# Keeping VectorE off the port it shares with GpSimd: operand places, engine choice and a new order in a fused attention and MLP kernel

## The chip, the cores and the metric

The kernel runs on one core of a Trainium2 chip. The metric is the device time of one execution in microseconds; for the kernel before, three runs gave 625.87, 627.99 and 629.17 us, with a median of 627.99 us. A profile was taken of a further execution.

Five engines work in parallel, each through its own queue in program order: TensorE (PE, with its weight loads shown as PEld), VectorE (DVE), ScalarE (ACT), GpSimd (POOL) and SyncE (SP), which here issues all transfers between HBM and SBUF. Products go to tiles in PSUM, of which the kernel keeps eight; here VectorE and ScalarE read them, and no GpSimd instruction does. Everything else lies in SBUF.

## The reference

The input x has 2048 rows of 512 values. Two blocks follow one another, each with a layer norm that is scaled and shifted by rows computed from a condition vector c.

```python
mod = (silu(c) @ w_mod).reshape(1, 6, 1, 512)      # sa, ca, ga, sb, cb, gb
h = layernorm(x) * (1 + ca) + sa
x = x + ga * A(h)
h = layernorm(x) * (1 + cb) + sb
x = x + gb * B(h)

def A(h):                                           # 32 heads of 16
    q, k, v = split(h @ wqkv)
    phi_q = concat(softmax(q @ w_phi), softmax(-(q @ w_phi)))    # per head, 32 features
    phi_k = concat(softmax(k @ w_phi), softmax(-(k @ w_phi)))
    o = (phi_q @ (phi_k.T @ v)) / (phi_q @ sum(phi_k) + 1e-6)
    return o @ wo

def B(h):
    g = gelu(layernorm(h) @ w1)                     # 512 wide
    x1 = h + shift(g) @ w2                          # quarters shifted by +1, -1, +2, -2 rows
    return x1 + gelu(layernorm(x1) @ w3) @ w4       # 1376 wide
```

## The kernel before, in words

The rows are worked on in tiles of 128. Matrix products run with each operand split into a rounded high part and a rest (`hi_lo`), and three products per pair of parts (`three`); the high part is a copy on ScalarE, and the rest is a subtraction, on VectorE or GpSimd.

There are three stages, which overlap at their edges:

- **Stage 1**, eight chunks of 256 rows. `h_chunk` normalises two tiles (`layernorm2`, from the second chunk on), transposes them on TensorE and splits them. `k_feat` and `v_feat` project keys and values, `q_feat` the queries, each with a softmax of both signs. Keys: `k_feat` divides the exponentials by their sums (tile `ke`), `kv_add` multiplies them with the values into the PSUM tile `kva` and adds the tiles up in `zacc`, a constant tile that the profile calls `const`. Queries: `q_feat` turns 32 by 32 blocks of the PSUM result into the SBUF tile `qt`, forms maximum and minimum, subtracts them into `qe`, and stores `qe` to HBM.
- **Stage 2**, `phase_a` and `mix`, eight chunks. `q_phi` loads a query tile (`e`), multiplies it with the summed keys (`ez`), forms the denominators in small tiles, scales `e` and turns it into `pT`; then come the products with `kvb` (`num`), with `wo`, two norms (`moments`), `w1` with a gelu (`gf`, `sh`), and, for the chunk before, `w2`. Between the stages, `zacc` goes through a product with ones, whose result `zbc` every `ez` needs.
- **Stage 3**, `phase_b`, four blocks of 512 rows: a norm, `w3` with a gelu in eleven column blocks (`up`), `w4` (`down`), and the sum with the two residuals (`xb`, `xc`).

No order is written by hand. `Plan` records every instruction with its cost, its tiles and its alternatives on other engines, and then `order` runs a list scheduler over all of them: at each step it takes, over the engines, the instruction that can start first; among those within a window the smallest number of program position plus `PRIO` of its group. `PICK` and `BIAS` add a handicap to an engine where an instruction may run on two, `CAP` limits how many tiles of a name live at once, `SLOTS` how many buffers of a size there are. What comes out is fixed at build time: which engine, and which place in its queue. Groups are named by part and tile ("h5" is the norm and split of chunk 5, "k11" the keys of tile 11, "z" the summed keys).

The scheduler knows one resource besides the engines and the buffers. An operation marked `lock`, and every GpSimd operation, waits for a variable `port` and then holds it:

```python
            if o.lock:
                port = end - (140 if o.eng == "Pool" else 0)
```

On VectorE that mark is set for `tensor_tensor` and `scalar_tensor_tensor` with both tensors in SBUF, for `tensor_scalar` of more than one element per row with input and output in SBUF, and for the VectorE alternative of an `act` between SBUF tiles. Each of these touches a line that the profile names: L397 and L399 are `tt` on VectorE and GpSimd, L407 `ts`, L415 `stt`, L420 `red`, L423 `recip`, L382 every `act`, L389 its alternatives, L538 and L522 the reciprocal square roots on GpSimd, L703 `turn`, L426 and L430 loads and stores, L447 and L456 products and transposes.

The norm of a pair of tiles (`moments`, then the caller) is a chain over three engines: sums of rows on ScalarE; `nm`, minus the mean, on VectorE; the sums of squares on ScalarE; `mv`, the variance, on VectorE; the root `rs` on GpSimd; `nm` times `rs` on VectorE; and the normalised tile on ScalarE.

## Time and profile before

| | |
|---|---|
| median of three runs | 627.99 us (625.87 to 629.17) |
| the profiled execution, device time | 632.06 us |
| its span, first to last instruction | 630.3 us |
| busy: PE, DVE, ACT, POOL | 602.3, 394.1, 290.3, 289.4 us |
| instructions: DVE, ACT, POOL | 715, 523, 234 |
| mean granted TensorE clock | 0.981 |
| moved through HBM | 47.78 MB read, 20.97 MB written |

The profiled execution is 1.8 us longer than its own span and 4.1 us longer than the median run. The span falls into a start (0 to 21 us, until the large products begin), stage 1 (to about 187 us, where the first `num` product starts), stage 2 (to about 373 us) and stage 3. A row of a timeline gives start, duration, engine, line, operation, tiles and shapes; "x8" is eight instructions in a row, and the bracket says how long the engine had been idle and what ended that. Two products are recorded for each product of two float32 operands.

### The profile page before, as it was taken

Reading aid. Unit: us, or ns where it says so; the run is one execution under the profiler, and the core shown is the slowest. Engines: PE = TensorE matmul, PEld = TensorE weight load, DVE = VectorE, ACT = ScalarE, POOL = GpSimd, SP = SyncE. Lnnn points to the kernel's source line nnn. Section 1 sums busy time; section 2 is a strip of 40 time slices with the busy share of each in tenths; the row PEclk is TensorE's granted clock in tenths of the full one; section 3 lists DMA queues with packets and bytes.
Section 4 is the critical chain, followed back from the end, with each engine's and each line's share of the span. In section 5 each row is a group of like instructions: output and inputs, shape, how many; then the busy total and the mean of one; then the engine's idle time right before and its main releaser. Section 6 shows DMA issues by size and latency. Waiting matters only on the chain.

```text
span 630.3 us, 9391 instructions
## 1 busy us (share of the span) xinstructions
PE 602.3 (96%) x3528; PEld 508.0 (81%) x3528; DVE 394.1 (63%) x715; ACT 290.3 (46%) x523; POOL 289.4 (46%) x234
## 2 busy tenths in 40 slices
PE   4999989998989999898998999999999999999997
PEld 4788868887878777686787988988888898888885
DVE  5689999888999999999975569314511321112112
ACT  3999477733333684553565565323422222221130
POOL 3358985597587689575445673100700060002000
PEclk9699999999999999999999899999999999999999
DMA  8853532201165525551354575102500140003001
GB/s 290 295 159 98 204 105 77 74 1 51 68 234 181 189 105 188 182 174 53 118 167 124 162 238 187 34 1 80 171 1 0 58 145 0 1 1 116 1 0 68
DMA packets 33854, 69.37 MB, mean 110 GB/s; under 512 B 4144, under 2 KB 4784, under 8 KB 33808
## 3 DMA queue, kind: packets, MB, share of 16 engines
q1 hardware_dynamic: 33808, 68.76, 32.7%
q8 instruction: 28, 0.46, 0.3%
q14 instruction: 18, 0.15, 0.1%
HBM read 47.78 MB, written 20.97 MB: 109 GB/s over the span
## 4 chain that ended last, share of the span: by engine, by line
PE 64%; DVE 21%; DMA 5%; ACT 4%; issue 3%; POOL 2%; SPq 1%; DVEq 0%; POOLq 0%
PE pp L447 39%; PE pa L447 22%; DMA xl<-dram 2%; DVE q L420 2%; DVE k L420 2%; PE pt L456 2%; DVE pz L420 2%; DVE pT L703 1%; DVE nm L407 1%; DVE ke L397 1%; DVE e L397 1%; ACT xn L382 1%; PE kva L447 1%; POOL w L399 1%; DVE q L415 1%
## 5 line engine op out<-in xcount | busy, mean ns | idle before, releaser
L447 PE MATMUL pp<-w,gg 128*128 128x512 f32 (+1 forms) x528 | 129.9, 396 | 0.4 <-DVE gg L397 0.4
L397 DVE TENSOR_TENSOR gg<-g,gg 128x512 fp32r<-128x512 f32 (+1 forms) x44 | 33.7, 766 | 152.1 <-ACT gg L382 152.1
L447 PEld LDWEIGHTS pp<-w,gg 128*128 128x128 f32 (+1 forms) x528 | 97.7, 188 | 22.8 <-DVE gg L397 0.8
L447 PE MATMUL pp<-w,hh 128*128 128x512 f32 x384 | 96.3, 407 | 0.9 <-ACT hh L382 0.9
L382 ACT ACTIVATE g<-pa 128x512 f32<-128x512 f32 (+1 forms) x44 | 26.2, 597 | 147.9 <-PE pa L447 147.9
L399 POOL TENSOR_TENSOR xb<-xb,gb 128x512 f32<-128x512 f32 x15 | 20.3, 1354 | 153.1 <-DMA xb<-dram 113.0
L447 PEld LDWEIGHTS pp<-w,hh 128*128 128x128 f32 x384 | 73.1, 194 | 19.0 <-issue 1.3
L447 PEld LDWEIGHTS pa<-bH,w 128*128 128x128 f32 (+1 forms) x528 | 64.9, 186 | 1.8
L447 PE MATMUL pa<-bH,w 128*128 128x256 f32 (+1 forms) x528 | 65.7, 281 | 0.0
L447 PE MATMUL pa<-bT,w 128*128 128x512 f32 (+1 forms) x264 | 64.3, 393 | 0.0
L447 PEld LDWEIGHTS pa<-bT,w 128*128 128x128 f32 (+1 forms) x264 | 48.8, 185 | 11.9
L447 PEld LDWEIGHTS pa<-nT,w 128*128 128x128 f32 x384 | 48.8, 195 | 3.9 <-issue 1.9
L447 PE MATMUL pa<-nT,w 128*128 128x256 f32 x384 | 50.9, 290 | 0.4 <-DVE nT L397 0.4
L447 PE MATMUL pp<-hh,w 128*128 128x256 f32 x384 | 49.2, 284 | 0.0
L447 PEld LDWEIGHTS pp<-hh,w 128*128 128x128 f32 x384 | 47.3, 189 | 2.1 <-issue 1.1
L447 PE MATMUL pp<-w,sh 128*128 128x512 f32 x192 | 48.8, 399 | 0.1
L447 PE MATMUL pp<-w,oT 128*128 128x512 f32 x192 | 47.6, 395 | 0.0
L399 POOL TENSOR_TENSOR w<-raw,w 128x512 fp32r<-128x512 f32 x26 | 36.3, 1403 | 16.6 <-ACT w L382 15.8
L447 PEld LDWEIGHTS pp<-w,sh 128*128 128x128 f32 x192 | 34.8, 188 | 9.0 <-issue 1.3
L447 PEld LDWEIGHTS pp<-w,oT 128*128 128x128 f32 x192 | 35.1, 188 | 7.9 <-issue 0.8
L399 POOL TENSOR_TENSOR e<-e,q 128x1024 f32<-128x1024 f32 x13 | 26.3, 2024 | 25.3 <-DVE q L397 25.2
L399 POOL TENSOR_TENSOR ez<-e,const 128x1024 f32<-128x1024 f32 x15 | 36.1, 2408 | 1.2 <-ACT const L382 0.9
(130 smaller groups left out, 1005.5 us busy)
## 6 DMA issues: line engine op xcount, KB each, us to landing
xl<-in_x SPq DMA_DIRECT2D x32, 256.0 KB, 3.3
dram<-qe SPq DMA_DIRECT2D x16, 512.0 KB, 2.9
e<-dram SPq DMA_DIRECT2D x16, 512.0 KB, 4.5
raw<-in_w SPq DMA_DIRECT2D x26, 256.0 KB, 3.2
mod<-in_wmod SPq DMA_DIRECT2D x24, 256.0 KB, 4.7
dram<-xl SPq DMA_DIRECT2D x16, 256.0 KB, 2.1
xc<-dram SPq DMA_DIRECT2D x16, 256.0 KB, 4.0
dram<-h SPq DMA_DIRECT2D x16, 256.0 KB, 2.7
```

Source lines behind the costliest of these rows:

```text
L382: nc.scalar.activation(o(), i(), func, **kw)
L397: dve = ("DVE", 71 + 1.04 * o.n, lambda: nc.vector.tensor_tensor(o(), a(), b(), op=op))
L399: pool = ("Pool", cost, lambda: nc.gpsimd.tensor_tensor(o(), a(), b(), op=op))
L407: plan.op(eng, cost, lambda: e.tensor_scalar(o(), a(), get(s1), get(s2), op0=op0, **kw), [o], [a] + ptr, lock=o.n > 1 and not isps(a) and ...
L415: nc.vector.scalar_tensor_tensor(o(), a(), get(s), b(), op0=op0, op1=op1, **kw)
L420: plan.op("DVE", 65 + 1.04 * a.n, lambda: nc.vector.tensor_reduce(o(), a(), axis=AX.X, op=op), [o], [a])
L447: nc.tensor.matmul(o(), a(), b(), start=s, stop=e, **kw)
L456: nc.tensor.transpose(o(), i(), ident())
L703: plan.op("DVE", 71 + 1.04 * o.n, lambda: nc.vector.transpose(o(), i()), [o], [i])
```

## The change

Six things change together.

1. Past the first chunk of the norms (the list `apart` is filled once `h_chunk(0)` is recorded), a `tt` between SBUF tiles that might have run on either engine goes to GpSimd always, and an `act` between SBUF tiles has no VectorE alternative any more.
2. The small steps of the norms move from VectorE to ScalarE: `small` writes `nm`, `mv` and, one column at a time, the product of `nm` and `rs`.
3. Queries of the tiles with an even number keep `qt` in SBUF, and their two subtractions run on GpSimd; those with an odd number are turned in place in PSUM, and the subtractions run on VectorE from there.
4. The small factor 1e-6 enters the denominators by one operation on the PSUM tile `pz`, in place of two operations on small SBUF tiles.
5. The gelu in `up` writes back to its PSUM tile, and both parts are taken from there; the SBUF tile `g` is gone.
6. `CAP`, `PRIO`, `PICK` and `BIAS` have new numbers throughout, so every engine's order is new. `SLOTS`, the costs and the rules of the scheduler are as they were.

```diff
-CAP = {"const": 64, "bd": 3, "raw": 2, "pp": 9, "xl": 2, "st": 12, "mv": 81, "rs": 9, "nm": 31, "xn": 42, "acc": 9,
+CAP = {"const": 69, "bd": 6, "raw": 2, "pp": 8, "xl": 2, "st": 24, "mv": 32, "rs": 16, "nm": 41, "xn": 37, "acc": 3,
...
-PRIO = {"b0": -16, "b1": -397, "b2": 357, "e0": 3, "e10": 23, "e11": -177, "e12": 193, "e13": 150, "e14": -413, "e15":
+PRIO = {"b0": -2, "b1": 349, "b2": 219, "b3": 72, "e0": 361, "e1": -282, "e10": -85, "e11": -11, "e12": -303, "e13":
...
-BIAS = {"DVE": -1158, "Pool": -1352, "window": 55, "ADVE": 1217, "AActivation": 0, "APool": 3308, "start": 1,
-        "halves": 0, "late": 4, "ln_act": [1, 2, 3, 4, 5, 6, 7], "pair": [0, 1, 2, 3, 4, 5, 6, 7]}
+BIAS = {"DVE": 2046, "Pool": 10, "window": 59, "ADVE": 54, "AActivation": 0, "APool": 1259, "start": 1, "halves": 0,
+        "late": 4, "ln_act": [1, 2, 3, 4, 5, 6, 7], "pair": [0, 1, 2, 3, 4, 5, 6, 7], "qpool": [0, 2, 4, 6, 8, 10, 12,
+        14]}
...
+    apart = []
...
+        if alts and apart and not isps(i) and not isps(o):
+            alts = [e for e in alts if e != "DVE"]
...
+        if eng == "any" and lock and apart:
+            eng = "Pool"
...
+    def small(o, i, scale, bias=0.0):
+        ptr = [scale] if isinstance(scale, V) else []
+        plan.op("Activation", 110 + 93 * len(ptr),
+                lambda: nc.scalar.activation(o(), i(), AF.Copy, scale=get(scale), bias=bias), [o], [i] + ptr)
...
-        ts(nm, total, -1.0 / D, None, OP.mult, None)
+        small(nm, total, -1.0 / D)
...
-        ts(sq, sq, 1.0 / D, EPS, OP.mult, OP.add)
+        small(sq, sq, 1.0 / D, EPS)
...
+    def shift_of(nm, r):
+        nmr = T("nm", [P, nm.n])
+        for i in range(nm.n):
+            small(nmr[:, i:i + 1], nm[:, i:i + 1], r[:, i:i + 1])
+        return nmr
...
-        tt(nmr, nm, r, OP.mult)
+        nmr = shift_of(nm, r)
...
-        q = T("qt")
-        turn(q, p.re("p i t -> p (i t)", (D,)))
-        softmax_in(e, mm, q, "any")
+        p = p.re("p i t -> p (i t)", (D,))
+        pool = c * TPC + j in BIAS["qpool"]
+        q = T("qt") if pool else p
+        turn(q, p)
+        softmax_in(e, mm, q, "Pool" if pool else "DVE")
...
     hh0 = h_chunk(0)
+    apart.append(True)
...
-        stt(t2, sm0, 1e-6, sm1, OP.mult, OP.mult)
...
+        stt(a2[:, :, 0], sm2[:, :, 0], 1e-6, a2[:, :, 0], OP.mult, OP.add)
+        tt(u, a2, swap, OP.mult)
         red(den, u, OP.add)
-        tt(den, den, t2, OP.add)
...
-            g = T("g", [P, QB])
-            act(g[:n, :], p[:n, :], AF.Gelu_apprx_tanh)
+            act(p[:n, :], p[:n, :], AF.Gelu_apprx_tanh)
             gg = T("gg", [P, 2, QB], FR)
-            hi_lo(gg[:n, 0, :], gg[:n, 1, :], g[:n, :])
+            hi_lo(gg[:n, 0, :], gg[:n, 1, :], p[:n, :])
```

Counted over the built programs, VectorE has 588 instructions in place of 683, ScalarE 521 in place of 459 and GpSimd 266 in place of 234 (an accumulator's read is not counted here); TensorE has the same 3290 products and transposes, and SP the same 235 transfers. Three places of the new order follow.

**VectorE before, in stage 1 around the norm of chunk 5** (`nm`, `mv` are the norm's small tiles, `ke` and `k` the keys and their sums, `q` and `e` those of the queries):

```order
L397 TENSOR_TENSOR nm_932<-nm_679,rs_854 128x2
L423 RECIPROCAL k_203_929<-k_203_929 128x64
L420 TENSOR_REDUCE k_200_910<-pp_865 128x32
L397 TENSOR_TENSOR ke_956<-pp_865,k_200_910 128x32x16
L397 TENSOR_TENSOR ke_956<-k_200_910,pp_865 128x32x16
L397 TENSOR_TENSOR ke_905<-ke_905,k_203_929 128x1024
L407 TENSOR_SCALAR nm_968<-st_958 128x2
L415 SCALAR_TENSOR_TENSOR q_214_970<-q_190_860 128x32
L420 TENSOR_REDUCE q_215_980<-e_834 128x64
L420 TENSOR_REDUCE k_217_993<-ke_956 128x64
L407 TENSOR_SCALAR mv_983<-mv_983 128x2
```

and ScalarE in the changed program, at the norm of the same chunk:

```order
L386 ACTIVATE xn_850,st_826<-xl_798 128x512
L386 ACTIVATE qe_845<-qe_845 128x1024
L553 ACTIVATE nm_860<-st_826 128x2
L386 ACTIVATE xn_827,mv_863<-xl_792,nm_860 128x512
L386 ACTIVATE vv_877<-pp_832 128x512
L386 ACTIVATE xn_850,mv_863<-xl_798,nm_860 128x512
L553 ACTIVATE mv_863<-mv_863 128x2
L553 ACTIVATE nm_929<-nm_860,rs_911 128x1 x2
L386 ACTIVATE xn_827<-xl_792,nm_929,rs_911 128x512
```

The steps `nm` and `mv` now stand in ScalarE's own queue, next to the passes over the tile that they serve; VectorE has none of them.

**GpSimd before, from the last `zacc` addition that it makes to the first scaled queries** (`const_631` is `zacc`, `const_1608` is `zbc`):

```order
L399 TENSOR_TENSOR const_631<-const_631,ke_1412 128x1024
L399 TENSOR_TENSOR w_1590<-raw_1484,w_1508 128x512
L399 TENSOR_TENSOR w_1590<-raw_1488,w_1508 128x512
L399 TENSOR_TENSOR w_1590<-raw_1592,w_1508 128x512
L399 TENSOR_TENSOR ez_1648<-e_771,const_1608 128x1024
L399 TENSOR_TENSOR qe_1671<-qt_1664,q_327_1666 128x32x16
L399 TENSOR_TENSOR qe_1671<-q_327_1666,qt_1664 128x32x16
L399 TENSOR_TENSOR ez_1697<-e_834,const_1608 128x1024
L399 TENSOR_TENSOR w_1590<-raw_1602,w_1508 128x512
L399 TENSOR_TENSOR e_771<-e_771,q_340_1733 128x1024
L399 TENSOR_TENSOR e_834<-e_834,q_356_1817 128x1024
```

and in the changed program, from the first `ez` to the fourth scaled query tile (`const_1643` is `zbc`):

```order
L405 TENSOR_TENSOR ez_1675<-e_745,const_1643 128x1024
L405 TENSOR_TENSOR ez_1696<-e_775,const_1643 128x1024
L405 TENSOR_TENSOR ez_1732<-e_857,const_1643 128x1024
L405 TENSOR_TENSOR e_745<-e_745,q_335_1734 128x1024
L405 TENSOR_TENSOR qe_1775<-qt_1769,q_340_1772 128x32x16
L405 TENSOR_TENSOR qe_1775<-q_340_1772,qt_1769 128x32x16
L405 TENSOR_TENSOR ez_1839<-e_1797,const_1643 128x1024
L405 TENSOR_TENSOR e_775<-e_775,q_348_1821 128x1024
L405 TENSOR_TENSOR e_857<-e_857,q_359_1867 128x1024
L405 TENSOR_TENSOR e_1797<-e_1797,q_367_1916 128x1024
```

All four tiles are multiplied and scaled on GpSimd now, where VectorE took one `ez` and three of the sixteen scalings before; and TensorE has the `num` products of these four tiles next to one another, where it had three before.

**SP before, in the start, around the four slices of the value weights** (`raw<-in_wv`; `mod` are slices of `w_mod`, `xl` tiles of x):

```order
L426 DMA mod_189<-in_wmod 128x512
L426 DMA raw_200<-in_wv 128x512
L426 DMA mod_205<-in_wmod 128x512
L426 DMA mod_208<-in_wmod 128x512
L426 DMA mod_217<-in_wmod 128x512
L426 DMA raw_231<-in_wv 128x512
L426 DMA mod_247<-in_wmod 128x512
L426 DMA raw_254<-in_wv 128x512
L426 DMA xl_260<-in_x 128x512
L426 DMA xl_268<-in_x 128x512
L426 DMA raw_287<-in_wv 128x512
```

and in the changed program, between the first slice and the last:

```order
L434 DMA mod_199<-in_wmod 128x512
L434 DMA mod_211<-in_wmod 128x512
L434 DMA mod_216<-in_wmod 128x512
L434 DMA mod_232<-in_wmod 128x512
L434 DMA mod_237<-in_wmod 128x512
L434 DMA raw_246<-in_wv 128x512
L434 DMA xl_251<-in_x 128x512
L434 DMA xl_255<-in_x 128x512
L434 DMA raw_270<-in_wv 128x512
L434 DMA mod_283<-in_wmod 128x512
L434 DMA mod_294<-in_wmod 128x512
L434 DMA raw_316<-in_wv 128x512
```

The first slice stands at the same place in the queue in both; the last one has three more transfers ahead of it, and the last slice of the key weights, earlier in the queue, two.

## The prediction

> **What bounds the kernel now.** I read the table of stretches first, cut at the stages. Each row gives the stretch, its length, busy time with (instructions) of PE, PEld, DVE, ACT and POOL, then the granted clock, the transfers' share and their GB/s.

> ```profile
> 0.00:21.00 21.00, 11.95 (x56) 10.58 (x56) 11.26 (x29) 10.85 (x23) 5.95 (x16) 0.81 0.89 314
> 21.00:187.00 166.00, 159.61 (x1034) 134.84 (x1036) 152.70 (x223) 103.52 (x190) 122.26 (x75) 0.97 0.36 117
> 187.00:373.00 186.00, 177.70 (x1070) 146.48 (x1067) 157.35 (x333) 102.22 (x192) 122.37 (x110) 0.98 0.45 152
> 373.00:631.00 258.00, 253.09 (x1375) 216.12 (x1373) 72.78 (x133) 73.71 (x120) 38.82 (x34) 1.00 0.18 59
> ```

> TensorE sets the end. In stage 3 it is busy 253 of 258 us at full clock, so no other engine can shorten it, and the few microseconds left are the last tile's sum and store, which the change does not touch. In stages 1 and 2 TensorE idles 166 − 159.6 = 6.4 us and 186 − 177.7 = 8.3 us, together 14.7 us. VectorE is busy there for 92% and 85% of the time, GpSimd for 74% and 66%. What can be won lies in these two stages, and it is small against 630 us: the idle time, and what it costs in clock.

> Next the timeline, at each idle time of TensorE above 0.5 us past the start, with the VectorE row that made it late:

> ```profile
> 83.48 5.71 POOL L399 TENSOR_TENSOR const<-const,ke 128x1024 f32<-128x1024 f32 x2
> ...
> 86.88 2.33 DVE L407 TENSOR_SCALAR nm<-st 128x2 f32<-128x2 f32 x1
> ...
> 91.39 1.80 PE L447 MATMUL kva<-ke,vv 128*64 128x128 f32 x16 [2.40 <-ACT vv L382]
> ...
> 147.06 2.29 DVE L397 TENSOR_TENSOR const<-const,ke 128x1024 f32<-128x1024 f32 x1
> ...
> 152.93 1.52 PE L447 MATMUL pp<-const,const 128*128 128x512 f32 x3 [1.64 <-DVE const L397]
> ...
> 179.89 1.63 DVE L415 SCALAR_TENSOR_TENSOR q<-q 128x32 f32<-128x32 f32 x1
> ...
> 181.44 2.36 DVE L397 TENSOR_TENSOR e<-e,q 128x1024 f32<-128x1024 f32 x1
> ...
> 186.71 1.54 PE L447 MATMUL pp<-pT,const 128*64 128x256 f32 x8 [2.20 <-DVE const L397]
> ...
> 262.37 2.40 DVE L407 TENSOR_SCALAR nm<-st 128x2 f32<-128x2 f32 x1
> ...
> 265.98 1.08 PE L447 MATMUL pp<-pT,const 128*64 128x256 f32 x8 [1.66 <-DVE pT L703]
> ...
> 283.60 1.65 DVE L407 TENSOR_SCALAR nm<-st 128x2 f32<-128x2 f32 x1
> ...
> 288.40 1.08 PE L447 MATMUL pp<-pT,const 128*64 128x256 f32 x8 [0.72 <-DVE pT L703]
> ...
> 291.62 3.36 DVE L397 TENSOR_TENSOR e<-e,q 128x1024 f32<-128x1024 f32 x1
> ...
> 295.64 0.65 PE L456 MATMUL pt<-const,n 128*128 128x128 f32 x4 [1.12 <-DVE oT L397]
> ...
> 297.46 0.63 PE L456 MATMUL pt<-const,n 128*128 128x128 f32 x4 [1.16 <-DVE h L397]
> ...
> 344.84 0.69 DVE L526 BATCH_NORM_STATS2 st<-xl 128x6 f32<-128x512 f32 x1 [2.40 <-DMA xl<-dram]
> ...
> 346.70 0.66 PE L456 MATMUL pt<-const,n 128*128 128x128 f32 x4 [2.13 <-ACT n L382]
> ```

> The eight PE rows add up to 2.40 + 1.64 + 2.20 + 1.66 + 0.72 + 1.12 + 1.16 + 2.13 = 13.0 us, nearly the whole 14.7. Seven of the eight have the same cause ahead of them. A step on two numbers per row (`nm`) lasts 2.33, 2.40 or 1.65 us; the first ends at 89.21, when the two GpSimd instructions that began at 83.48 end (89.19). An addition into `zacc` lasts 2.29, a small factor (`q<-q`) 1.63, a scaling of `e` 2.36 and 3.36 us. VectorE waits inside its instruction until GpSimd lets go, and everything behind it in the queue is late, until a product is. In the eighth, VectorE stands 2.40 us before a statistic of stage 3 whose load has not landed; the `nm` times `rs` that TensorE's transposes need is queued behind it.

> The third part is the clock. Read by slices of 16 us it is full in stages 1 and 2 after 32 us, but for three:

> ```profile
> 80.00:96.00 16.00, 13.60 (x91) 10.83 (x90) 16.00 (x21) 11.49 (x23) 13.42 (x8) 0.89 0.32 99
> ...
> 176.00:192.00 16.00, 13.80 (x122) 11.26 (x117) 15.78 (x24) 5.64 (x9) 16.00 (x11) 0.89 0.49 175
> ...
> 336.00:352.00 16.00, 13.87 (x83) 12.64 (x83) 8.78 (x23) 7.12 (x14) 7.11 (x9) 0.89 0.44 140
> ```

> Each holds one of the idle times above 2 us (at 91, 187 and 347), and each lost 0.11 × 16 = 1.76 us, 5.3 us together. The gaps of 1.64 and 1.66 us show no such dip. [...]

> So 13.0 + 5.3 = **18.3 us** hang on VectorE's waits.

> **The change, part by part.**

> *Norm steps, factor, additions: off VectorE.* The prices before:

> ```profile
> L407 DVE TENSOR_SCALAR nm<-st 128x2 f32<-128x2 f32 x23 | 10.3, 450 | 0.6 <-ACT xn L382 0.5
> ...
> L415 DVE SCALAR_TENSOR_TENSOR q<-q 128x32 f32<-128x32 f32 x16 | 8.6, 539 | 0.0
> ...
> L382 ACT ACTIVATE const<-const 128x4 f32<-128x4 f32 x1 | 0.2, 205 | 2.4 <-DMA const<-in_c 2.4
> ```

> The 23 `nm` rows average 450 ns, with 2.4 at most; the 16 factors 539 ns. On ScalarE the nearest row is an ACTIVATE of 4 numbers per row, 205 ns. I count 23 + 23 + 30 = 76 new ones there (the products one column at a time), 76 × 0.205 = 15.6 us; they are all new there, so the bounds are 0 and, for those with a second operand at twice the row, 76 × 0.41 = 31 us. ScalarE idles 166 − 103.5 and 186 − 102.2, together 146 us, which hides them; without that cover they would cost themselves. They stand between passes that ScalarE makes itself, so each norm loses two changes of engine and gains none. The wait for `rs` from GpSimd moves from VectorE's queue to ScalarE's, where the exponentials of `ke` and `qe` are now behind it; what waits for those is GpSimd, below.
> [...]

> With the additions to `zacc`, the scalings and `ez` gone too, no VectorE instruction past the first chunk has two large SBUF tensors or a norm step; what is left reads PSUM or one SBUF tile. I take **−18.3 us** for the eight waits, all seven with GpSimd in them and the eighth because its `nm` step now stands on ScalarE. Bounds: 0 (each late product finds another reason) and −20.0 (all 14.7 and the 5.3).

> *What arrives at GpSimd.* Rows of the groups:

> ```profile
> L399 POOL TENSOR_TENSOR ez<-e,const 128x1024 f32<-128x1024 f32 x15 | 36.1, 2408 | 1.2 <-ACT const L382 0.9 <-DMA e<-dram 0.4
> ...
> L399 POOL TENSOR_TENSOR ke<-ke,k 128x1024 f32<-128x1024 f32 x14 | 27.2, 1946 | 11.7 <-ACT hh L382 6.4 <-DVE k L423 5.1
> ...
> L399 POOL TENSOR_TENSOR e<-e,q 128x1024 f32<-128x1024 f32 x13 | 26.3, 2024 | 25.3 <-DVE q L397 25.2
> ...
> L399 POOL TENSOR_TENSOR const<-const,ke 128x1024 f32<-128x1024 f32 x10 | 24.9, 2486 | 1.5 <-DVE nm L397 1.2
> ...
> L399 POOL TENSOR_TENSOR w<-raw,w 128x512 fp32r<-128x512 f32 x26 | 36.3, 1403 | 16.6 <-ACT w L382 15.8 <-PE pp L447 0.8
> ...
> L399 POOL TENSOR_TENSOR qe<-q,qt 128x512 f32<-128x512 f32 x13 | 14.3, 1104 | 0.0
> ```

> By instruction counts: 5 more `const` × 2.486, 3 `e` × 2.024, 1 `ez` × 2.408, 2 `ke` × 1.946, 13 `w` × 1.403, and 10 fewer `qe` × 1.104: +32.0 us. Another 2 `acc`, 6 `raw`, 5 `sh` and 2 `xb`, 512 numbers a row like `w`, are bounded by the rows of `qe` and `w`: 15 × 1.1 to 1.4, 17 to 21 us. So GpSimd goes from 289 to about 340 us, nearly all in stages 1 and 2, where it had 352 − 244.6 = 107 us idle. It fits, with half the room.

> Two places could be too tight. For them:

> ```profile
> L447 PE MATMUL pp<-w,hh 128*128 128x512 f32 x384 | 96.3, 407 | 0.9 <-ACT hh L382 0.9
> ...
> L447 PE MATMUL pp<-hh,w 128*128 128x256 f32 x384 | 49.2, 284 | 0.0
> ...
> L447 PE MATMUL kva<-ke,vv 128*64 128x128 f32 x256 | 16.8, 284 | 2.4 <-ACT vv L382 2.4
> ...
> 33.43 1.94 POOL L399 TENSOR_TENSOR ke<-ke,k 128x1024 f32<-128x1024 f32 x1 [3.15 <-DVE k L423]
> ...
> L703 DVE STREAM_TRANSPOSE pT<-e 128x1024 f32<-128x1024 f32 x16 | 19.7, 1234 | 0.0
> ```

> *First, the product of `zacc` (group z).* TensorE blocks there until the last addition. GpSimd's first `ke` started at 33.43. From there to that addition the new order has 16 `ke` (31.1 us), 15 `const` (37.3), 6 `qe` (6.6), 6 `w` (8.4), 9 `acc` and 4 `raw` as `w` (18.2), five roots and a copy (between half a `w` and a whole one each, 4 to 8): 107 us. That ends at 33.4 + 107 = 140.5 without a pause. TensorE was ready for it at 152.93 − 1.64 = 151.3; less the 4.2 us lost at 91, plus one more key group ahead (12 × 96.3/384 = 3.0), it is ready near 150. GpSimd may pause 9.5 us on the way. I take **0**, with the row of 1.64 as the upper bound of this forecast; more is the first rival.

> *Second, the first `num` products.* From z on GpSimd has two `qe` and two `w` (5.0 us, which also cover `zbc`), then the ten rows shown, 4 × 2.408 + 4 × 2.024 + 2 × 1.104 = 19.9, and VectorE a turn of 1.23: 26.2 us. TensorE has meanwhile 48 products of 512 columns (12.0), 96 of 256 (96 × 49.2/384 = 12.3) and 32 of `kva` (2.1): 26.4. That is a dead heat, and all four tiles are wanted at once. I take a gap of 2 us and half a dip of the clock, **+2.9**; bounds 0 and the 2.20 + 1.76 of before.

> *Queries of odd tiles.* 16 subtractions of 512 numbers come to VectorE; by half of the turn of 1024 (0.62 us) they are 10 us, against 10.3 + 8.6 of the two groups above that leave. The turn into PSUM has no row; between that half and the whole I take the half. The cover is VectorE's idle time, 352 − 310 = 42 us before and more now; without it TensorE would pay these 10. **0**.

> *Gelu in place.* Its PSUM tile is now held through three instructions:

> ```profile
> L382 ACT ACTIVATE g<-pa 128x512 f32<-128x512 f32 x40 | 23.9, 597 | 132.7 <-PE pa L447 132.7
> ```

> That is 3 × 0.6 = 1.8 us in place of 0.6. A column block takes TensorE 24 products of 512 columns, 6.0 us by the rows above, and there are four such tiles beside the four sums; **0**, and 1.2 us a block if the tiles ran out.

> *The start.* Here the transfers bind:

> ```profile
> 16.00:32.00 16.00, 14.70 (x54) 11.40 (x54) 11.12 (x22) 15.43 (x32) 6.14 (x5) 0.66 0.89 295
> ```

> At 295 GB/s a slice of 0.262 MB takes 0.89 us. The last key weights have two more ahead, the last value weights three: 1.8 to 2.7 us later. TensorE uses part of that for the transposes of chunk 1, brought forward (about 1 us). I take **+1**; bounds 0 and +2.7.

> *Small gaps.* The 14.7 − 13.0 us that are not among the eight stay, and I allow **+1** for places that the new order makes.

> **The sum**: −18.3 + 0 + 2.9 + 1 + 1 = −13.4. The profiled execution took 632.06, so its like would take 618.7; from the median of 627.99 it is 614.6. If the 4.1 us between the two are stalls that the median run did not have, only 618.7 is left. I take the middle, **617 us**, with 611 to 623 as this case's own range.

> **The rivals.**

> *GpSimd takes VectorE's place (slower).* GpSimd was idle for 26% of stage 1 and for 16% of the slice from 80 us, waiting for keys, turns and loads. If it pauses a fifth of the time in its new queue, 107 us take 107/0.8 = 134, and z comes at 167 in place of 150: 17 us late, and a dip of 1.8. Then 614.6 to 618.7 becomes 633 to 638. It decides from 9.5 us of pauses on; it breaks even with the gain at some 23. For it: GpSimd serves its queue in order, and keys wait there for sums, exponentials and VectorE. Against: that idle time came with less work; the additions to `zacc` are spread between the keys and fill pauses.
> [...]

> *Waits change their place.* The seven port waits go, but half of the late products are late for the next reason: an in-order queue elsewhere, a buffer, a load. Half of 18.3 stays: 614.6 + 9.2 to 618.7 + 9.2, 624 to 628, within what can be told from no change or just beyond. For it: VectorE stays the second busiest engine, and every queue is new. Against: only one of the eight had such a reason before.

> *The waits go wholly.* Both dead heats are won, the start costs nothing: 18.3 to 19.7 us, 608 to 612.

> *It does not do what it says*: some VectorE instruction still waits in stages 1 and 2. The remaining forms (reductions, turns, subtractions from PSUM) show no such stretching before; I give it no chance of its own beyond the second rival's.

> **How the numbers follow.** Forecast 0.60, GpSimd paces stage 1 0.14, waits change place 0.18, all gone 0.08. A difference of 0.5%, 3.1 us, is about what a measurement of this kernel tells from none: 624.9 and 631.1 are the borders. Faster: 0.59 + 0.08 + a third of 0.18 = 0.73. Slower: 0.11 of the first rival's 0.14. Same: the rest, 0.16. The range reaches from the best case, 610, into the second rival and to the border of the first, 630.

> **What would show it.** Right: no VectorE row of `nm`, and the small rows of `q`, the reductions and turns with one duration each; TensorE idle below 6 us between 21 and 373; at most one slice there below clock 0.95; GpSimd near 340 us busy. The first `num` row tells the dead heat, the row of ones times `zacc` the first rival: idle there with GpSimd's `const` as releaser. Wrong: TensorE idle as before in sum, at other rows; or GpSimd's queue without a pause up to z and z late.

## The result, and the profile after

The changed kernel took 610.28 us in the median (four runs, 609.93 to 614.54), the kernel before beside it 628.45 us (four runs). The ratio is 0.9734 with a 95% interval of 0.9682 to 0.9785: 2.7% faster. The forecast was 617 us, 610 to 630.

The profiled execution took 609.93 us and its span is 608.2 us. The table of stretches of the kernel after, cut at the same places as before; the columns are stretch, length, busy time with (instructions) of PE, PEld, DVE, ACT and POOL, granted clock, transfers' share and GB/s:

```profile
0.00:21.00 21.00, 11.39 (x58) 10.94 (x59) 13.48 (x31) 10.57 (x23) 9.29 (x19) 0.89 0.88 314
21.00:187.00 166.00, 164.10 (x1084) 138.49 (x1083) 136.86 (x216) 104.81 (x208) 142.65 (x90) 0.99 0.36 121
187.00:373.00 186.00, 185.74 (x1165) 158.37 (x1165) 135.44 (x277) 116.76 (x251) 129.74 (x121) 1.00 0.50 164
373.00:608.00 235.00, 231.32 (x1227) 196.17 (x1225) 53.17 (x98) 61.92 (x104) 42.99 (x39) 1.00 0.16 52
```

Between 21 and 373 us TensorE idles 1.90 + 0.26 = 2.16 us; before it was 14.7. The other columns can't be compared row by row, since the same cuts hold different work: the first `num` product starts at 178.23 us now (before at 186.71), the first `w3` product at 349.72 (372.87). Over the whole span VectorE's busy time fell from 394.1 to 338.9 us, GpSimd's rose from 289.4 to 324.7, and ScalarE's from 290.3 to 294.1.

The timeline of the kernel after holds two idle times of TensorE above 0.2 us past the start. Here is the larger with the ScalarE rows ahead of it, and the two places for which the prediction feared a wait, the product of `zacc` with ones (`pp<-const,const`) and the first `num` products (`pp<-pT,const`):

```profile
70.00 0.63 ACT L386 ACTIVATE xn<-xl 128x512 f32<-128x512 f32 x1 [1.62 <-DMA xl<-in_x]
70.54 0.18 ACT L386 ACTIVATION_READ_ACCUMULATOR xn<-xl 128x1 f32 x1
70.63 0.58 ACT L386 ACTIVATE vv<-pp 128x512 f32<-128x512 f32 x1
...
71.26 1.09 PE L455 MATMUL kva<-ke,vv 128*64 128x128 f32 x16 [1.90 <-ACT vv L386]
...
145.68 2.39 POOL L405 TENSOR_TENSOR const<-const,ke 128x1024 f32<-128x1024 f32 x1
...
149.35 1.88 PE L455 MATMUL pp<-const,const 128*128 128x512 f32 x4
...
178.23 3.67 PE L455 MATMUL pp<-pT,const 128*64 128x256 f32 x32
```

No bracket stands at 149.35 or at 178.23: TensorE came there straight from other work. GpSimd's last addition ended at 145.68 + 2.39 = 148.07, 1.28 us ahead of the product. The gap at 71 is a new one: ScalarE stood at a tile of x that had not landed, and the copy of the values `vv`, which was due, stood behind it in the queue.

The groups of the kernel after that answer to the prices of before (mean ns stands behind the busy time; the first row is the 128x512 form alone):

```profile
L405 POOL TENSOR_TENSOR w<-raw,w 128x512 fp32r<-128x512 f32 x34 | 43.6, 1295 | 14.7 <-ACT w L386 9.2 <-PE pp L455 4.1 <-PE pa L455 1.2
L405 POOL TENSOR_TENSOR const<-const,ke 128x1024 f32<-128x1024 f32 x14 | 33.5, 2396 | 0.3
L405 POOL TENSOR_TENSOR acc<-acc,mod 128x512 f32<-128x512 f32 x12 | 15.4, 1285 | 1.5 <-ACT acc L386 0.7 <-ACT mod L386 0.6
...
L553 ACT ACTIVATE nm<-nm,rs 128x1 f32<-128x1 f32 x30 | 7.2, 286 | 11.1 <-POOL rs L546 11.1
L722 DVE STREAM_TRANSPOSE pp<-pp 128x512 f32<-128x512 f32 x8 | 5.7, 715 | 0.7 <-PE pp L455 0.7
...
L403 DVE TENSOR_TENSOR qe<-q,pp 128x512 f32<-128x512 f32 x8 | 5.4, 676 | 0.0
...
L553 ACT ACTIVATE mv<-mv 128x2 f32<-128x2 f32 x23 | 4.6, 200 | 0.5
L553 ACT ACTIVATE nm<-st 128x2 f32<-128x2 f32 x23 | 4.6, 199 | 7.9 <-DVE h L423 7.8
...
L423 DVE SCALAR_TENSOR_TENSOR pz<-q,pz 128x32 f32<-128x32 f32 x16 | 3.1, 191 | 0.3
```

`nm` costs 199 ns on ScalarE where VectorE's rows averaged 450, and the factor on PSUM 191 where it was 539.

The clock: of the slices of 16 us up to 384 us only one is below full, and it lies at the edge of the start. Beside it stands the one that holds the gap of 1.90 us; the slice behind that is at 1.00 too:

```profile
16.00:32.00 16.00, 14.98 (x68) 13.05 (x69) 13.27 (x25) 15.65 (x36) 11.26 (x11) 0.79 0.84 297
64.00:80.00 16.00, 14.11 (x84) 11.67 (x84) 13.62 (x19) 12.60 (x29) 14.02 (x11) 1.00 0.73 246
```

Span against span, 630.3 − 608.2 = 22.1 us. TensorE's idle time in the span (span less busy time) went from 28.0 to 15.7 us, 12.3 of them; the clock (share not granted times span) from 0.019 × 630.3 = 12.0 to 0.007 × 608.2 = 4.3 us, 7.7 of them; 2.1 us are in neither and stay open.

### The profile page after: what moved, and what is told of

It reads as the page before. It is cut to its first block, busy times and chain, and to the rows that moved or that the text cites. A ratio compares the mean times of both kernels' runs of the same rounds, so it can differ in the third digit from the quotient of the medians.

```text
span 608.2 us, 9374 instructions
## 1 busy us (share of the span) xinstructions
PE 592.5 (97%) x3528; PEld 504.0 (83%) x3528; DVE 338.9 (56%) x620; ACT 294.1 (48%) x585; POOL 324.7 (53%) x266
## 4 chain that ended last, share of the span: by engine, by line
PE 86%; DMA 5%; ACT 3%; POOL 2%; issue 1%; DVE 1%; SPq 1%; POOLq 0%; DVEq 0%
PE pp L455 54%; PE pa L455 27%; PE pt L464 3%; PE kva L455 2%; DMA mod<-in_wmod 2%; DMA xl<-in_x 1%; DMA dram<-qe 1%; ACT xn L386 1%; POOL w L405 1%; DMA raw<-in_wv 1%; SPq L434 1%; ACT ke L386 0%; ACT w L386 0%; POOL sh L405 0%; ACT qe L386 0%
## 5 line engine op out<-in xcount | busy, mean ns | idle before, releaser
L403 DVE TENSOR_TENSOR gg<-pa,gg 128x512 fp32r<-128x512 f32 (+1 forms) x44 | 30.3, 689 | 152.3 <-ACT gg L386 152.3
L386 ACT ACTIVATE pa<-pa 128x512 f32<-128x512 f32 (+1 forms) x44 | 25.6, 581 | 147.4 <-PE pa L455 147.3
L455 PE MATMUL pp<-w,hh 128*128 128x512 f32 x384 | 93.0, 399 | 0.0
L455 PEld LDWEIGHTS pp<-w,hh 128*128 128x128 f32 x384 | 71.6, 189 | 17.2 <-issue 1.2
L405 POOL TENSOR_TENSOR w<-raw,w 128x512 fp32r<-128x512 f32 (+2 forms) x39 | 48.7, 1259 | 18.1 <-ACT w L386 12.6
L455 PEld LDWEIGHTS pa<-nT,w 128*128 128x128 f32 x384 | 47.4, 189 | 2.5 <-issue 0.8
L455 PE MATMUL pa<-nT,w 128*128 128x256 f32 x384 | 48.5, 283 | 0.0
L405 POOL TENSOR_TENSOR ez<-e,const 128x1024 f32<-128x1024 f32 x16 | 38.4, 2405 | 5.8 <-DMA e<-dram 3.8
L405 POOL TENSOR_TENSOR ke<-ke,k 128x1024 f32<-128x1024 f32 x16 | 30.8, 1939 | 11.7 <-DVE k L431 8.1
L405 POOL TENSOR_TENSOR const<-const,ke 128x1024 f32<-128x1024 f32 x14 | 33.5, 2396 | 0.3
```

Of the source, the lines that this page charges most:

```text
L386: nc.scalar.activation(o(), i(), func, **kw)
L403: dve = ("DVE", 71 + 1.04 * o.n, lambda: nc.vector.tensor_tensor(o(), a(), b(), op=op))
L405: pool = ("Pool", cost, lambda: nc.gpsimd.tensor_tensor(o(), a(), b(), op=op))
L455: nc.tensor.matmul(o(), a(), b(), start=s, stop=e, **kw)
```

## The experiments

The theory of the port, as the scheduler calls it: VectorE's instructions that it marks wait for a running instruction of GpSimd, and the change gains what those waits cost. The trace before shows such waits: of the 61 norm steps on two numbers (`nm`, `mv`, `nm` times `rs`; median 0.16 us) ten took 0.34 to 2.40 us, the others 0.28 at most, and each of the ten ended 0.01 to 0.03 us after a GpSimd instruction that ran beside it. The 32 reductions of `qt`, without the mark, took 642 to 690 ns. The theory's rivals: the norms gain because ScalarE keeps their chain on one engine; or the gain is the new order, which the new numbers make, and not the new instructions.

### The norm steps back on VectorE, in two forms

The changed kernel was run once more beside its variants. In the first variant `nm` and `mv` are VectorE instructions on two numbers per row again, in the second the same steps are two instructions on one number each. Order and all else are the changed kernel's.

```diff
     def small(o, i, scale, bias=0.0):
-                lambda: nc.scalar.activation(o(), i(), AF.Copy, scale=get(scale), bias=bias)
+                # first form, where scale is a constant:
+                lambda: nc.vector.tensor_scalar(o(), i(), scale, bias, op0=OP.mult, op1=OP.add)
+                # second form, where scale is a constant:
+                lambda: [nc.vector.tensor_scalar(o[:, j:j + 1](), i[:, j:j + 1](), scale, bias, ...) for j in range(o.n)]
```

> The changed kernel once more, as the reference for its two variants on the same chip: 610 us, between 607 and 613, by every theory.

> The changed kernel with its own order, but nm and mv (46 steps, two numbers per row) are written by VectorE again, each in one instruction; nothing else differs, and every queue but these two keeps its rows. Theory of the port: GpSimd is busy 143 of 166 and 130 of 186 us, so most of the 46 meet a running GpSimd instruction and last up to 2.4 us; VectorE's rows for them average 0.6 us or more (450 ns before), gaps of TensorE above 0.5 us come back, and the kernel takes 613 to 622 us. Theory that the norms gain because ScalarE keeps the chain on one engine: slower as well, by the same 3 to 12 us, but with VectorE's rows near 0.2 us and gaps after ScalarE. Theory that only the new order counts: 610 us, within 2.

> As the run with nm and mv on VectorE, but each step in two instructions on one number per row, whose rows before never showed a wait (191 to 216 ns). Theory of the port: 610 us, within 2, although VectorE issues 46 instructions more and the chain changes engines as often as in the other variant. Theory of the chain on one engine: as slow as that variant, 613 to 622 us. Theory of the order: 610 us, within 2.

| kernel | median of 4, us | ratio to before, 95% |
|---|---|---|
| changed, again | 610.57 | 0.9705 (0.9657 to 0.9753) |
| steps on two numbers, VectorE | 621.22 | 0.9868 (0.9819 to 0.9917) |
| steps on one number, VectorE | 612.95 | 0.9737 (0.9687 to 0.9787) |

The summary of the tile `nm` on VectorE (count, then minimum, median and maximum in ns, first and last start), for the form with two numbers:

```profile
L553 DVE TENSOR_SCALAR nm<-st x23: 126/550/1694, 15.4 to 335.7; 128x2 f32<-128x2 f32 x23
```

for the form with one number:

```profile
L553 DVE TENSOR_SCALAR nm<-st x46: 97/143/155, 15.2 to 327.9; 128x1 f32<-128x1 f32 x46
```

and for the kernel before:

```profile
L407 DVE TENSOR_SCALAR nm<-st x23: 119/169/2405, 16.9 to 339.3; 128x2 f32<-128x2 f32 x23
```

The largest gaps of TensorE, in the form with two numbers:

```profile
204.12 1.36 PE L464 MATMUL pt<-const,n 128*128 128x128 f32 x8 [1.60 <-ACT n L386]
...
243.68 1.08 PE L455 MATMUL pp<-pT,const 128*64 128x256 f32 x8 [0.93 <-DVE h L403]
...
295.28 1.36 PE L464 MATMUL pt<-const,n 128*128 128x128 f32 x8 [1.77 <-ACT n L386]
...
341.30 1.36 PE L464 MATMUL pt<-const,n 128*128 128x128 f32 x8 [1.04 <-ACT n L386]
```

With two numbers per row the `nm` steps have a median of 550 ns and last up to 1.69 us, and gaps come back, most of them where the normalised tile `n` is transposed: 10.7 us lost in the median. In the profiled executions (619.26 against 611.19 us) TensorE idles 7.8 us between 21 and 373 us where it idled 2.0. With one number per row none lasts over 155 ns, though there are twice as many instructions and the chain changes engines just as often, and the time is that of the changed kernel within what can be told. So what these two steps gain on ScalarE is that they no longer wait for the port; that it shortens the chain is not needed. The single-number form did nearly as well on VectorE here (612.95 us beside 610.57).

A second thing stands in these rows. Before, the median of the 23 steps was 169 ns: the planner, which reckons with the port, had put most of them where they met no wait, and a few long ones (five of 0.34 to 2.40 us) did the harm. In the changed kernel's order, which was not made for them, the median is 550.

### One part alone, in the old order

Three kernels keep the old numbers and, for the first two, each instruction's old place in the program. The first only issues the norm steps on ScalarE. The second only issues on GpSimd what the planner had given to VectorE although GpSimd could take it, past the first chunk. The third does both, and takes the denominators from PSUM.

```diff
+    def moved(o, i, s1, s2):                      # planned as VectorE's, issued on ScalarE
+        plan.op("DVE", 71 + 0.55 * o.n, lambda: nc.scalar.activation(o(), i(), AF.Copy, scale=s1, bias=s2), [o], [i], lock=True)
...
-        ts(nm, total, -1.0 / D, None, OP.mult, None)
+        moved(nm, total, -1.0 / D, 0.0)
...
         for o in self.order():
-            o.fn()
+            if o.eng == "DVE" and o.lock and o.i >= self.apart and "Pool" in o.alts:
+                o.alts["Pool"][1]()               # second and third kernel: issued on GpSimd
+            else:
+                o.fn()
```

> The kernel before, every queue in its old order, with only the norm steps (nm, mv, nm times rs) taken from VectorE's queue and put at the same place of the program into ScalarE's. Theory of the port: the waits of nm go, with the gaps at 91, 266, 288 and 347 us (2.40, 1.66, 0.72, 2.13 us) and two of the three clock dips (1.76 us each), so 10 us less than before at the most; 618 to 625 us. Theory that only the new order counts: as before, 626 to 630 us. Theory that ScalarE's queue in an order not made for the steps only moves the waits (the changed code under the old numbers took 634 us, with gaps after ScalarE's n and nT): 628 to 636 us.

> The kernel before in its old order, with only those additions and products between SBUF tiles past the first chunk that the planner had given to VectorE, although GpSimd could take them, put into GpSimd's queue at the same place of the program. Theory of the port: the zacc and e rows of VectorE go, with the gaps at 153, 187, 296 and 297 us (1.64, 2.20, 1.12, 1.16 us) and one dip, 8 us at most, while nm's remain; but GpSimd gets some 20 us more to do in an order not made for it, so that new gaps after GpSimd may eat it: 620 to 633 us. Theory that only the new order counts: 628 us or more, since a longer GpSimd queue can then only cost.

> Both of the last two and the denominators from PSUM, in (nearly) the old order: the changed instructions, without the numbers. Theory of the port: VectorE has no wait left past the first chunk, and if the order matters little, 612 to 618 us; if GpSimd's and ScalarE's queues in the old order bring waits of their own, about as the changed code under the old numbers, 634 us. Theory that only the new order counts: 628 us or more.

| kernel, old order | median, us | ratio to before, 95% |
|---|---|---|
| norm steps on ScalarE | 623.67 | 0.9922 (0.9897 to 0.9947) |
| additions on GpSimd | 634.63 | 1.0104 (1.0052 to 1.0157) |
| both, and denominators | 643.72 | 1.0231 (1.0182 to 1.0280) |

The norm steps alone gain 5 us. The gaps at 266 and 288 us are gone and those at 91 and 347 are down to 1.0. Of those that the prediction put down to VectorE's additions and scalings, the two at 153 and 187 are still there, while the two near 296 are gone (none is above 0.5 us there), so these hung on the order of events as well:

```profile
89.96 1.09 PE L447 MATMUL kva<-ke,vv 128*64 128x128 f32 x16 [1.04 <-ACT mv L542]
...
151.41 1.96 PE L447 MATMUL pp<-const,const 128*128 128x512 f32 x4 [1.65 <-DVE const L397]
...
185.14 2.81 PE L447 MATMUL pp<-pT,const 128*64 128x256 f32 x24 [2.15 <-DVE const L397]
...
337.56 0.65 PE L456 MATMUL pt<-const,n 128*128 128x128 f32 x4 [1.00 <-ACT n L382]
```

Moving the additions alone costs 6 us. In that kernel the waits that `zacc` made on VectorE stand behind GpSimd now, and at z the wait is longer (3.57 us, before 1.64):

```profile
154.58 3.78 PE L450 MATMUL pp<-const,const 128*128 128x512 f32 x4 [3.57 <-POOL const L402]
...
344.95 0.66 PE L459 MATMUL pt<-const,n 128*128 128x128 f32 x4 [2.49 <-ACT n L385]
```

The norm's steps on VectorE wait about as much as before: `nm` came down (350 ns in the mean, before 450), `mv` and the product with `rs` went up (296 and 427, before 265 and 240), together 21.2 in place of 20.0 us.

With both, no VectorE row of stages 1 and 2 has two SBUF tensors or a norm step on two numbers, and the kernel is the slowest of the three, by 10 us above what the theory of the port allowed at the most (634). Its products wait for GpSimd's queue and for ScalarE's:

```profile
110.60 0.33 PE L459 MATMUL pt<-const,xn 128*128 128x128 f32 x1 [2.75 <-ACT xn L385]
...
157.76 1.98 PE L450 MATMUL pp<-const,const 128*128 128x512 f32 x4 [3.38 <-POOL const L402]
...
354.85 5.91 PE L450 MATMUL pp<-w,sh 128*128 128x512 f32 x13 [2.44 <-POOL sh L402]
```

In the old order, then, taking the norm steps off the port gains 5 us, and moving the additions to GpSimd as well costs more than the free port gains. These runs change two things at once for the additions, the port and the length of GpSimd's queue; the gaps behind GpSimd say that the second is what costs. The theory of the port, as I had put it, holds for the norm steps and fails for the additions in the old order.

### The code without the numbers, and the numbers without the code

Here the planner works anew, once with the changed code and the old CAP, PRIO, PICK and BIAS, once with the old code and the new ones.

```diff
-CAP, PRIO, PICK, BIAS = those of the changed kernel
+CAP, PRIO, PICK, BIAS = those of the kernel before, with "qpool" as in the changed kernel   # changed code
...
-CAP, PRIO, PICK, BIAS = those of the kernel before
+CAP, PRIO, PICK, BIAS = those of the changed kernel, with CAP["g"] = 19                     # code before
```

> The changed kernel with the numbers of the kernel before (CAP, PRIO, PICK, BIAS; the even queries on GpSimd), so the planner orders the new instructions by priorities made for the old ones. Theory of the port: VectorE has no waits past the first chunk whatever the order, so the eight gaps' 13 us and the dips' 5.3 mostly go, but GpSimd's queue gets longer in an order not made for it, and some gaps after GpSimd come: 612 to 622 us. Theory that only the new order counts: 628 us or more.

> The kernel before with the new CAP, PRIO, PICK and BIAS, planned anew: the old instructions under the new numbers. Theory of the port: VectorE's rows for nm, zacc and e wait again for GpSimd (means of 450 ns and more for nm), and TensorE has at least the 13 us of gaps of before: 628 to 645 us. Theory that only the new order counts: 610 to 615 us.

The changed code under the old numbers took 633.74 us (ratio 1.0076, 1.0051 to 1.0101); the old code under the new numbers 691.27 us (1.0985, 1.0911 to 1.1059). Each half alone makes the kernel slower, by 5 and by 62 us; together they make it 18 us faster. Neither theory holds for both. For the first kernel the port gave 612 to 622 us, and what came is what the rival of the order gave, 628 or more. For the second that rival gave 610 to 615, and falls; the theory of the port gave 628 to 645 there with means of 450 ns and more for `nm`, and they were 292.

In the changed code under the old numbers stage 1 is good, TensorE busy 164.46 of 166 us, but stage 2 idles 14 us, mostly in gaps behind ScalarE, and three clock dips there cost 6.8 us:

```profile
205.45 1.36 PE L463 MATMUL pt<-const,n 128*128 128x128 f32 x8 [1.77 <-ACT n L385]
208.23 6.00 PE L454 MATMUL pa<-nT,w 128*128 128x256 f32 x24 [1.42 <-ACT nT L385]
...
339.04 0.38 PE L454 MATMUL pa<-nT,w 128*128 128x256 f32 x1 [2.25 <-ACT nT L385]
```

In the old code under the new numbers the worst place comes where stage 2 begins. TensorE waits 15.64 us for `num`, and VectorE ahead of it waits for the port three times in a row: the first of these instructions ends at 205.43, GpSimd's `ez` beside it (2.34 us from 203.05) at 205.39. The first two take 0.18 us at 213.59 and 215.97, and the third 1.18 at 214.87:

```profile
203.72 1.71 DVE L416 SCALAR_TENSOR_TENSOR q<-q 128x32 f32<-128x32 f32 x1
205.36 1.29 DVE L398 TENSOR_TENSOR q<-q,q 128x32 f32<-128x32 f32 x1
206.58 2.33 DVE L398 TENSOR_TENSOR ez<-e,const 128x1024 f32<-128x1024 f32 x1
...
213.59 0.18 DVE L416 SCALAR_TENSOR_TENSOR q<-q 128x32 f32<-128x32 f32 x1
...
215.97 0.18 DVE L398 TENSOR_TENSOR q<-q,q 128x32 f32<-128x32 f32 x1
```

That is the chain whose small steps and `ez` the changed code has taken off the port. How much of the 62 us is the port and how much a planner under foreign numbers was not separated.

### How near GpSimd is to pacing stage 1

The changed kernel with more additions on GpSimd, whose result nobody uses: two or four ahead of the last addition into `zacc`, or sixteen spread over the middle of stage 1. Nothing else changes.

```diff
             tt(zacc, first[0] if tt_ == 1 else zacc, e, OP.add, "any")
+            # more = 2 or 4 where tt_ == NT - 1; or 2 where 4 <= tt_ < 12; issued ahead of the addition
+            [nc.gpsimd.tensor_tensor(extra[:], e[:, :D](), e[:, :D](), op=OP.add) for _ in range(more)]
```

> The changed kernel with two more additions of 128x512 on GpSimd (1.29 us each by its rows, 2.6 us together, their result unused) ahead of the last addition into zacc. In the changed kernel that last addition ended at 148.07 us and the product with ones began at 149.35. Theory that GpSimd reaches z in a dead heat: the product is 2.6 less 1.3 = 1.3 us late, a gap of that length stands ahead of it, the clock stays full, and the time is 611 to 612 us. Theory that GpSimd has room there: no gap, 610 us.

> The same with four additions (5.2 us). Theory of the dead heat: a gap of 5.2 less 1.3 = 3.9 us ahead of the product with ones. Theory that gaps from about 2.1 us on bring a clock dip: the slice of 16 us behind it shows about 0.89 and 1.8 us more, 615 to 616 us; without a dip 614 us. Theory that GpSimd has room there: 610 us.

> The changed kernel with sixteen more additions of 128x512 (20.6 us), two ahead of each of eight additions into zacc in the middle of stage 1 (tiles 4 to 11). From 33.4 to 149.3 us GpSimd is busy 101 of 115.9 us, so 14.9 us are free. Theory that only GpSimd's sum counts: the product with ones is 20.6 less 14.9 less 1.3 = 4.4 us late, 615 us. Theory that its pauses cannot be used, since what it waits for comes late as well: up to 20.6 less 1.3 = 19.3 us late, 625 to 630 us, with gaps at the products of keys and values too.

The times are 611.44, 615.62 and 619.33 us (ratios 0.9736, 0.9806 and 0.9858; intervals 0.9708 to 0.9763, 0.9772 to 0.9840, 0.9832 to 0.9885). The additions were cheaper than I had priced them, 1.04 to 1.10 us each. The product of `zacc` with ones, with two, four and sixteen additions:

```profile
150.37 1.98 PE L455 MATMUL pp<-const,const 128*128 128x512 f32 x4 [0.72 <-POOL const L405]
```

```profile
145.26 4.38 POOL L756 TENSOR_TENSOR extra<-ke 128x512 f32<-128x512 f32 x4
...
151.99 3.78 PE L455 MATMUL pp<-const,const 128*128 128x512 f32 x4 [2.92 <-POOL const L405]
```

```profile
156.17 3.78 PE L455 MATMUL pp<-const,const 128*128 128x512 f32 x4 [6.10 <-POOL const L405]
```

Four additions take 4.38 us; less the 1.28 us of room that is 3.1, and the gap is 2.92. Two at the same price give 2.2 − 1.3 = 0.9, and the gap is 0.72. So the changed kernel reaches z with 1.3 us in hand and no more. Spread out, sixteen additions (16.7 us) make the product 156.17 − 149.35 = 6.8 us later: GpSimd's pauses between 33.4 us and the product took up some 8 us of them, from 14.9 down to 6.7 us. Neither extreme was right; about half of the pauses could be used.

The slice with the gap of 2.92 us, of the run with four additions, has a dip:

```profile
144.00:160.00 16.00, 13.08 (x62) 9.93 (x62) 5.78 (x9) 5.10 (x12) 15.19 (x13) 0.79 0.25 90
```

0.21 × 16 = 3.4 us of clock. Gap and dip are 6.3 us, of which the run lost 5 (the gap at 71 us was 0.60 there). That the time lies in the 615 to 616 us expected with a dip is luck: the gap was 1 us shorter than expected, and the dip twice as long.

### The new gap at 71 us

One pair of neighbours in ScalarE's queue changes places: the sums of the late tile of x go behind the copy of the values.

```diff
-        for o in self.order():
-            o.fn()
+        seq = self.order()
+        queue = [o for o in seq if o.eng == "Activation"]
+        # the first neighbours that are sums of a tile of x and then a copy into vv
+        ...
+        seq.remove(stat)
+        seq.insert(seq.index(vv) + 1, stat)
+        for o in seq:
+            o.fn()
```

> The changed kernel with one pair of neighbours in ScalarE's queue exchanged: the copy of the values vv that the product at 71.26 us waited for stands ahead of the sums of a tile of x whose load had not landed at 69 us. Theory that TensorE sets the end everywhere: the gap of 1.90 us is gone, and so is its time, 608 to 609 us; if the statistics behind it become late instead, 610 us.

608.73 us in the median (four runs, 607.83 to 608.93; ratio 0.9688, 0.9662 to 0.9714). The eight runs of the changed kernel lie between 609.5 and 614.54, above all four, but the kernel before was faster beside these four as well (627.78 us, beside the eight 628.45 and 629.50). The gap is gone from the timeline, and the product with ones begins at 148.10, where it had begun at 149.35:

```profile
148.10 1.88 PE L463 MATMUL pp<-const,const 128*128 128x512 f32 x4
```

Its span is 606.9 us, 1.3 us less. The gap that it removes is 1.90 us in the profile of the changed kernel and 1.08 in that of its repetition, so about 1 to 2 us are to be had. The trace shows that the gap is gone; that the time is shorter than the changed kernel's is not shown, since the intervals of the ratios overlap.

## Why the prediction was right, and where it was not

**The forecast as a whole**: right in direction and inside its range, but only just. 610.28 us lies 0.28 us above the lower end of 610, and outside the 611 to 623 that the prediction calls this case's own range. What came is the rival in which the waits go wholly (608 to 612 us: both dead heats won, the start at no cost), which had been given a chance of 0.08.

**What bounds the kernel**: right. TensorE sets the end, and what it idled in stages 1 and 2 was what could be won. Of 14.7 us it got back 12.5.

**The −18.3 us for the eight gaps and three dips**: right in size. All eight gaps are gone and so are the three dips. That the median fell by 18.2 us, from the 628.45 measured beside it, is nearly the same number by chance, since the start and the small gaps moved too. The variant with the norm steps back shows that the port is the cause for `nm` and `mv`, worth 10.7 us in the new order. For the additions, the scalings and the small factor no run puts them back alone in the new order, so their share is argued and not shown. And the mechanism was only half of it. The term names the new instructions as its whole reason, and the order does not occur in it; the runs without the new numbers show that the same instructions lose 5 us (planned anew by the old numbers) and nearly the same ones 15 us (in the old order). The step that failed is the sentence that took −18.3 "all seven with GpSimd in them" from the instructions alone and put rivals of order at 0.18 and 0.14. The 633 to 638 us of the rival in which GpSimd takes VectorE's place are what three of these kernels came near or passed (633.7, 634.6, 643.7), but not by its mechanism, a z that is 17 us late: the wait at z was 3.57 and 3.38 us in two of them, and the third had none. The 5.3 us for the dips came because the three gaps went; that a gap from 2.1 us on goes with a dip, as was supposed for the run with four additions, does not hold (last section).

**z at 0**: right, and narrow. TensorE was ready at 149.35 against an estimate near 150. GpSimd's first `ke` started at 35.95 us, 2.5 later than the 33.43 taken from before, and from there to the end of its last addition it paused 12.1 us where I allowed 9.5. It had room all the same, since its work to that point was 100 us, not the 107 of the estimate.

**The dead heat at `num`, +2.9**: wrong; it is the mis-sized term. There was no gap. Two of its parts were off. TensorE's cover from z to `num` was 178.23 − 149.35 = 28.9 us and not 26.4, mostly because I priced 32 products of `kva` by a row that counts two records for each (256 for the program's 128); the product with ones itself was left out as well:

```profile
162.34 1.97 PE L455 MATMUL kva<-ke,vv 128*64 128x128 f32 x32
...
169.99 1.97 PE L455 MATMUL kva<-ke,vv 128*64 128x128 f32 x32
...
177.86 1.24 DVE L722 STREAM_TRANSPOSE pT<-e 128x1024 f32<-128x1024 f32 x1
```

The two `kva` rows are 3.9 us where 2.1 stood in the sum. And the four tiles were not all wanted at once: the last turn (the third row) ended at 179.10, while TensorE was already on the products of the first tiles. The chain took 29.75 us in place of 26.2, because GpSimd had pauses in it that I had left out, so both sides were too short by some 3 us.

**The start, +1**: right for the position (the large products begin at 22.16, before at 21.15), not for the time. The clock in 16 to 32 us was 0.79 where it was 0.66, 2.1 us more than given up. The changed kernel's variants in its own order all show 0.79 there, the three kernels with changed instructions in the old order 0.66 to 0.68.

**Small gaps, +1**: beyond the eight, 1.7 us were left before; after there are 2.16 in all, 1.90 of them the new one at 71. So +0.5 and not +1, and for the kind of reason that I had given (an in-order queue and a load).

**ScalarE**: 15.6 us of small steps predicted, 4.6 + 4.6 + 7.2 = 16.4 measured, and hidden. **Turn into PSUM**: 715 ns; half of 1.23 was taken. The subtractions from PSUM took 0.67 each for 0.62. **Gelu in place**: the stage from the first `w3` product to the end took 608.2 − 349.72 = 258.5 us, before 630.3 − 372.87 = 257.4; nothing was won there, as the 0 said.

**GpSimd at 340 us**: 324.7. The rows that I multiplied held GpSimd's own waits for VectorE (one `acc` row took 2.30 us where the median was 1.30; last section). In the kernel after, `acc` fell from 1475 to 1285 ns, `const` from 2486 to 2396, and `w` of 128x512 from 1403 to 1295. Over the whole kernel the estimate was 15 too high, and some 12 of that, estimated from the means of the groups that both kernels have, are instructions that became shorter.

**The sum**: −13.4 from the profiled execution or from the median, 617 in the middle. Without the two terms that did not come (2.9 for `num`, 1 for small gaps, of which 0.5 came) it would have been −16.8, and with the start's gain in clock near −19. From the median of 627.99 that is 609 to 611. The choice of the middle between the two starting points cost 2 us: the 4.1 us by which the profiled execution was longer were not left in the changed kernel, whose profiled execution took 609.93. Profiled against profiled the fall is 22.1 us, and some 3 us of it are in none of the terms.

## What to carry to other kernels

An instruction on two numbers took 2.40 us here, where the shortest took 0.12, and ended with its neighbour's instruction, 25 ns behind it. Look for small rows whose longest is many times their median (here 2405 ns against 169), and try a form or an engine whose rows show no such wait (here one number, at most 155 ns, or ScalarE, 199 in the mean). How much that is worth depended on an order that fits the new durations: changed instructions under old priorities, and new priorities under old instructions, were both slower here than neither. And price a count of instructions only by a row that counts the same thing.

## What the runs showed of the hardware that was not expected

**The three clock dips of the kernel before have one length, and a gap's length alone did not decide them.** The expectation for four additions took gaps from 2.1 us on for dips. But with norm steps alone in the old order a gap of 2.15 us has no dip, and in the old order with both parts changed a gap of 3.38 us at 157.76 has none, while 2.92 us gave one of 3.4 us with four additions, and 1.77 and 1.42 us close together gave 0.80 in the slice from 208 us under the old numbers.

```profile
88.21:91.62 3.41, 1.01 (x12) 0.80 (x11) 3.41 (x6) 2.38 (x7) 2.23 (x2) 1.00 0.12 7
91.62:95.03 3.41, 3.41 (x21) 2.71 (x18) 3.41 (x4) 2.42 (x6) 2.59 (x2) 0.50 0.45 152
```

And two stretches of that length over which the gap of 3.38 us is spread:

```profile
152.66:156.08 3.42, 1.72 (x15) 1.51 (x13) 1.56 (x3) 0.66 (x1) 3.42 (x4) 1.00 0.00 0
156.08:159.49 3.41, 1.73 (x5) 0.87 (x5) 0.43 (x1) 1.47 (x5) 3.41 (x3) 1.00 0.63 210
```

In the first pair TensorE idled 2.40 us of one stretch, and the next one ran at half clock. In the second it idled 1.70 and 1.68 us, and the clock stayed full. Cut on its grid from 30 to 400 us, the kernel before has three stretches with more than 2 us of idle time (2.40, 2.20 and 2.13), and each is followed by a dip; the others hold 1.64 us or less, and none of them is. In the kernel after, 1.71 us of the gap of 1.90 lie in one such stretch, and it went without a dip. By these numbers the three dips of before were a matter of place as well as of length; what decides in general is not shown. With four additions the slice lost 3.4 us of clock, as much as two of the dips of before.

**Both sides pay for the port, and both show it in their rows.** GpSimd's additions of 512 numbers (`acc`) took 1277 to 2300 ns before, with a median of 1300, and 1267 to 1304 after, so a few long rows made the mean 190 ns higher. The longest began at 81.21 us, beside an addition of VectorE into `zacc` that ran from 81.10 to 82.36, and took 1.0 us more than the median.
